# Routed experts behind linear attention: the first expert's first stage in seven products for two groups, and twelve sums on GpSimd

## The chip, the cores and the metric

One core of a Trainium2 chip runs the whole kernel. The time is device microseconds of one execution; the median of several runs is compared. The engines have their own instruction queues and work them off in order: TensorE (PE, matmuls), VectorE (DVE), ScalarE (ACT), GpSimd (POOL) and SyncE (SP, which only starts DMAs here). An instruction that waits for another engine holds everything behind it in its own queue.

## The reference

Eight heads of linear attention give x of 4608 rows and 512 columns. Routing turns x @ w_gate into a table P of 4608 x 8 by eight rounds of row and column scaling. Eight experts follow, and P weights their sum:

```python
logits = x @ w_gate
P = np.exp(logits - logits.max())
for _ in range(8):
    P /= P.sum(1, keepdims=True) + 1e-09
    P /= P.sum(0, keepdims=True) + 1e-09
    P *= N / E
for e in range(E):
    h = np.maximum(x @ w1[e], 0.0)
    out += P[:, e:e + 1] * (h @ w2[e])
```

N = 4608, D = 512, E = 8, F = 1024.

## The kernel before

x lies transposed in SBUF (`xT`, bf16) in nine groups of 512 rows; groups 0 to 7 form four pairs. The first stage of an expert is x @ w1 with relu (tile `hT`), the second is hT @ w2 (into `acc`, one f32 tile per group). The loop over experts is the last and longest part, some 775 of 1030 us.

Expert 0 works plainly: `up0` makes a quarter of a group's first stage (8 matmuls of 512 columns, 32 for the group), and `down0` one chunk of 128 rows of the second stage (8 matmuls of 512 columns, four chunks to a group). In the text a chunk is one such `down0`. Some of expert 0's work fills the attention stage; the rest runs behind it, in a list (`fill`) that alternates quarters and chunks. Beside it, on DVE and PE, runs the routing loop (`routing`).

Experts 1 to 7 use seven products instead of eight per group, each of a quarter of the operands (Winograd's scheme). That needs sums and differences made ahead: of w1 and w2 (`sums_w`, eight a expert, 128x1024 in bf16), and of x (`pair_sums_x` for a pair, `sums_x` for group 8), which are written to DRAM (`Xd`) and loaded again for each expert by `load_x`. `up7` is the first stage: products x1 to x4, y1, w1, w2 for each half `fp`; ACT keeps a partial result in SBUF (`keep`, tile `U`), DVE adds it to another and clips at zero (`add`), and one result goes through relu on ACT. For a single group a product is 4 matmuls of 256 columns and there are two halves, so 56 in all; for a pair it is 2 matmuls of 512 columns and four halves. `down7` is the second stage in seven products. `ORDER` interleaves the `up7` of one group with the `down7` of an earlier one. The second expert's first pair has no earlier one, so its products stand alone.

The routing loop has eight rounds, each a chain over two engines: DVE multiplies the table by `c_bc` (L952), sums its rows (L955), takes the reciprocal (L957), multiplies again (L958), sums columns into `cs` (L961); PE adds `cs` over the partitions (a matmul of 8 columns with `colw`, in the tile `early`); DVE takes the reciprocal into `c_bc` (L966). Both multiplications read two tensors in SBUF, of 288 f32 elements a partition. After the last round P is complete. P weights each expert's output, and the outputs of expert 0 are scaled by it on ACT at the start of `down7` of expert 1.

The order on each engine is not written by hand. Each operation is recorded with a duration that the author gave it, and a list scheduler (`Plan.schedule`) starts whatever can start earliest; the result is fixed at build time. An operation with `shared=True` doesn't overlap another such one in that plan: DVE's sums (`sub`) and the routing's multiplications have it, and everything on GpSimd.

GpSimd scales v in the attention stage, starts the loads of weights, and in the expert loop adds `V` to `acc` (L1317).

Of the kernel before, what the change touches and what calls it, by code (L numbers as in the profile page):

```python
# [228 lines left out]
def kernel(  # L229
# [11 lines left out]
    nc = tc.nc  # L241
# [93 lines left out]
    for x in range(2):  # L335
# [16 lines left out]
        late["s_p"].tile([128, 2, 512], BF16, name="X", tag=f"X_{i}"))  # L352
    ring("s_p", [128, NT], FP32, "rr", 1)
    ring("s_p", [128, E], FP32, "cs", 1)
    ring("s_p", [128, E], FP32, "c_bc", 1)
# [409 lines left out]
    def up(w1, g, hT, fcs, n, r=(), w=()):  # L765

        for f0 in fcs[::n]:
            ph = new(f"P{n}")
            ht = hT[f0 // 2]
            for i in range(n):  # L770
                for dc in range(NP):
                    pe(512, lambda f=f0 + i, i=i, dc=dc, ph=ph: mm(
                        ph()[:, 512 * i:512 * i + 512], w1()[:, dc, f * 128:(f + 1) * 128],
                        xT[:, dc, g * 512:(g + 1) * 512], dc == 0, dc == NP - 1),
                        xkeys(g, dc) + [(w1, (f0 + i) // 2), *r], [ph, *w], [ht])
            act(512 * n, lambda f0=f0, ph=ph, ht=ht: nc.scalar.activation(
                out=ht()[:, f0 % 2:f0 % 2 + n, :].rearrange("p a b -> p (a b)"),
                in_=ph()[:, 0:512 * n], func=ACT.Relu, bias=0.0, scale=1.0),
                [ph], [(ht, f0 + i) for i in range(n)])

    def down(w2, hT, tss, r=()):
        py = new(f"P{len(tss)}")
        for i, ts in enumerate(tss):
            for fc in range(8):
                pe(512, lambda i=i, ts=ts, fc=fc: mm(
                    py()[:, 512 * i:512 * i + 512],
                    hT[fc // 2]()[:, fc % 2, ts * 128:(ts + 1) * 128],
                    w2()[:, fc, :], fc == 0, fc == 7),
                    [(hT[f // 2], f) for f in (range(8) if fc == 0 else (fc,))]
                    + [(w2, f) for f in range(4)] + [*r], [(py, i)])  # L790
        return py
# [11 lines left out]
    def down0(g, part):  # L803
        tss = (part,)
        py = down(W[0][1], hts[g], tss, akey(g))

        def keys(ts):
            return [("acc", g, ts)] + [("acc", g, ts, j) for j in range(2) if g >= 9]
        for i, ts in enumerate(tss):
            if ts % 2:  # L810
                act(512, lambda i=i, ts=ts: nc.scalar.activation(
                    out=acc[g][:, ts, :], in_=py()[:, 512 * i:512 * i + 512], func=ACT.Copy,
                    bias=0.0, scale=P[:, 4 * g + ts, 0:1] if g >= 9 else 1.0),
                    [(py, i)] + akey(g), keys(ts))
# [87 lines left out]

    def expert0(i):
        if i < 4 * NG:
            up0(i // 4, i % 4)
        down0(i // 4 - 1, i % 4)

    fill = range(4 * NA + 4, 4 * NG + 4)

    def swap():  # L910
# [26 lines left out]
    def routing():  # L937
        c_bc = None
        for it in range(8):
            rr, wv, cs, pc = new("rr"), new("T"), new("cs"), new("P1")  # L940
            lk = [("L", g) for g in range(NG)]
            if c_bc is None:
                def u():
                    return L
                uk = lk
            else:
                ub = new("T")
                uk = [ub]

                def u(ub=ub):  # L950
                    return table(ub)
                dve(288, lambda u=u, c=c_bc: nc.vector.tensor_tensor(  # L952
                    out=u(), in0=L, in1=c()[:, None, :].to_broadcast([128, NT, E]),
                    op=ALU.mult), lk + [c_bc], uk, shared=True)
            dve(288, lambda u=u, rr=rr: nc.vector.tensor_reduce(  # L955
# [3 lines left out]
                out=table(wv), in0=L, in1=rr()[:, :, None].to_broadcast([128, NT, E]),  # L959
                op=ALU.mult), lk + [rr], [wv], shared=True)  # L960
            dve(480, lambda wv=wv, cs=cs: nc.vector.tensor_reduce(  # L961
# [7 lines left out]
            out=P, in0=table(wv), in1=c()[:, None, :].to_broadcast([128, NT, E]), op=ALU.mult),  # L969
            [c_bc, wv], ["P"], shared=True)  # L970

    routing()
    grant("X", 4, {id(d): d for key in [("L", g) for g in range(NG)] + ["colw"]
                   for d in plan.readers[key]}.values())
    for i in fill:
        expert0(i)


# [36 lines left out]
    def sums_w(e, w1, w2):  # L1015

        eng = pool if e == 0 else dve

# [14 lines left out]
        def t(n):  # L1033
# [32 lines left out]
        return A, Bq  # L1066

    def xq(g, i, j):

        return lambda: xT[:, 2 * i:2 * i + 2, 512 * g + 256 * j:512 * g + 256 * j + 256]  # L1070
# [7 lines left out]

    def pair_sums_x(p):

        X = [new("S") for _ in range(4)]

        def x(n):
# [3 lines left out]
        for n, y, z, r in ((0, b12, b11, ["sums of x"]), (1, b22, x(0), [X[0]]),  # L1087
                           (2, b22, b12, []), (3, b21, x(1), [X[1]])):
            sub(dve, 1024, x(n), y, z, ALU.subtract,
                xkeys(2 * p) + xkeys(2 * p + 1) + ["late"] + r,  # L1090
                [X[n]] + (["sums of x"] if n == 1 else []))
            dma("SP", 1 << 18, 250, lambda n=n: nc.sync.dma_start(out=Xd[p][n], in_=x(n)()),
                [X[n]], [("Xd", p, n)])

    def sums_x(g):

        X = [new("S") for _ in range(2)]

        def x(n):
            return lambda: X[n // 2]()[:, n % 2 * 2:n % 2 * 2 + 2]  # L1100

        b11, b12, b21, b22 = xq(g, 0, 1), xq(g, 0, 0), xq(g, 1, 1), xq(g, 1, 0)
        for n, y, z, r in ((0, b12, b11, []), (1, b22, x(0), [0]), (2, b22, b12, []),
                           (3, b21, x(1), [1])):
            sub(dve, 512, x(n), y, z, ALU.subtract,
                xkeys(g) + ["late", "sums of x"] + [(X[i // 2], i % 2) for i in r]
                + ([(X[1], "slot")] if n == 2 else []),
                [(X[n // 2], n % 2)] + ([(X[1], "slot")] if n == 0 else []))
        for i in range(2):
            dma("SP", 1 << 18, 250, lambda i=i: nc.sync.dma_start(  # L1110
                out=Xd[4][i], in_=X[i]().rearrange("p (k a) b -> p k (a b)", k=2)),
                [(X[i], n) for n in range(2)], [("Xd", 4, i)])

    def load_x(p):
# [19 lines left out]

    def up7(A, p, X, H, r0):

        pair = p < 4
        nf = 4 if pair else 2
        gs = (2 * p, 2 * p + 1) if pair else (8,)
        xk = [k for g in gs for k in xkeys(g)]  # L1140

        def b(n):
            i, j = {"11": (0, 1), "21": (1, 1), "22": (1, 0)}.get(n, (0, 0))
            if n[0] != "t":
                if pair:
                    return lambda k: xT[:, 2 * i + k, 1024 * p + 512 * j:][:, 0:512], []
                return lambda k: xT[:, 2 * i + k, 4096 + 256 * j:][:, 0:256], []
            t = int(n[1]) - 1
            if pair:
                return lambda k: X[t]()[:, k, :], [X[t]]  # L1150
            return lambda k: X[t // 2]()[:, t % 2, 256 * k:256 * k + 256], [X[t // 2]]

# [51 lines left out]
        more = [("banks", 0), ("banks", 1)]  # L1204
        more += [k for n in ("s2", "s3", "22") for k in A[n][1]] + X + list(r0)
        def x1(fp):
# [201 lines left out]
    ORDER = "X1 x10 w10 x11 X2 x20 y10 x21 Z1 y11 X3 w11 x30 x31 x40 x41 w20 Y1 w21 X4 Z2".split()  # L1408
    END = "aX1 aY1 b2 aX2 aZ1 b3 aX3 aX4 b0 aZ2 b1".split()
    queue = []  # L1410

    def pop():
        if not queue:
            return None
        e, g, H, B7, w2 = queue.pop(0)
        if (e, g) == (E - 1, 7):
            return down8(e, g, H, w2)
        return down7(e, g, H, B7)

    for e in range(1, E):  # L1420
# [63 lines left out]
```

## Time and profile before

| | us |
|---|---|
| runs | 1028.88, 1030.8, 1033.5 (median 1030.8) |
| the profiled execution | 1030.37 |
| its span, first to last instruction | 1028.6 |
| PE busy in it | 1006.3 |
| DVE, ACT, POOL busy | 866.7, 706.6, 465.1 |
| attention ends, routing starts | about 206 |
| P complete | 244.5 |
| first product of the second expert | 253.7 |

The profiled execution lies within the spread of the runs, 0.4 us under their median. Times in the trace are counted from the span's start. A row of the timeline has start, length, engine, line, operation, output <- inputs with shapes, a count, and in brackets the idle time before it and what ended it. A row of the grouped view has line, engine, operation, operands and count, then busy time and the mean in ns of one, then idle time before. Matmuls overlap their neighbours, so PE's pace is read from the distance of starts.

### The profile page before, as it was taken

To read this page: it belongs to the slowest core of one execution; us is meant where nothing else is said; L and a number is where in the kernel's file an instruction comes from. 1 tells how busy PE (TensorE), PEld (TensorE's weight loads), DVE (VectorE), ACT (ScalarE), POOL (GpSimd) and SP (SyncE) were. 2 spreads that over 40 slices of the span, in tenths; PEclk is the share of its full clock that TensorE was granted. 3 is DMA by queue.
4 is the path that set the end of the run, shared out by engine and by line. 5 is a ranking of instruction groups with operands and counts; after the bars stand their busy time and mean duration, and the time that the engine had idled before them with its cause. 6 is when DMAs were issued, how large, how long until landed. Compare 5 with 4: busy or idle time off the path is not lost.

```text
span 1028.6 us, 21737 instructions
## 1 busy us (share of the span) xinstructions
PE 1006.3 (98%) x7838; PEld 690.2 (67%) x7958; DVE 866.7 (84%) x1860; ACT 706.6 (69%) x1569; POOL 465.1 (45%) x534
## 2 busy tenths in 40 slices
PE   7899999999999999999999999999999999999998
PEld 5666666644566766676667766676667666776665
DVE  7999998987877888888878888888879888888776
ACT  7999999835688866656666566655666666665663
POOL 5877765400244353444434454435443544443443
PEclk9999999999999999999999999999999999999999
DMA  9998995095411243121611161106111341203333
GB/s 258 177 169 143 183 163 95 11 224 145 83 42 42 63 91 74 42 63 41 124 42 41 34 122 56 52 28 122 43 43 62 70 95 42 58 26 83 141 126 124
DMA packets 124316, 93.77 MB, mean 91 GB/s; under 512 B 47456, under 2 KB 115872, under 8 KB 124208
## 3 DMA queue, kind: packets, MB, share of 16 engines
q1 hardware_dynamic: 90448, 68.44, 24.5%
q0 software_dynamic: 33680, 23.90, 16.6%
q8 instruction: 62, 1.02, 0.4%
q14 instruction: 46, 0.38, 0.1%
q10 hardware_dynamic: 80, 0.03, 0.0%
HBM read 94.98 MB, written 14.16 MB: 106 GB/s over the span
## 4 chain that ended last, share of the span: by engine, by line
PE 91%; DVE 4%; DMA 1%; issue 1%; ACT 1%; SPq 0%; POOL 0%; DVEq 0%; ACTq 0%
PE P L1130 40%; PE P L1164 31%; PE P L484 18%; PE P L683 1%; DVE acc L1303 1%; DVE hT L1194 1%; DMA acc<-in_q_dram 1%; DVE w L1013 1%; PE P L722 1%; DMA acc<-in_k_dram 1%; DVE m L476 0%; SPq L406 0%; PE P L688 0%; DVE S L1013 0%; ACT k L480 0%
## 5 line engine op out<-in xcount | busy, mean ns | idle before, releaser
L1317 POOL TENSOR_TENSOR acc<-acc,V 128x512 f32<-128x512 f32 x244 | 313.9, 1298 | 433.4 <-ACT V L1313 430.0
L1190 ACT COPY U<-P 128x512 f32<-128x512 f32 x378 | 216.1, 588 | 133.4 <-PE P L1164 68.9
L1313 ACT ACTIVATE V<-P 128x256 f32<-128x256 f32 x488 | 212.7, 476 | 122.1 <-PE P L1130 118.6
L1194 DVE CUSTOM_DVE_ANT_0 hT<-P,U 128x512 bf16<-128x512 f32 x378 | 252.1, 686 | 36.7 <-ACT U L1190 21.0
L1130 PEld LDWEIGHTS <-S 128*128 128x128 bf16 x1984 | 194.1, 98 | 53.2
L1303 DVE SCALAR_TENSOR_TENSOR acc<-P,acc 128x256 f32<-128x256 f32 x372 | 159.6, 477 | 71.7 <-PE P L1130 69.2
L1164 PE MATMUL P<-xT,w 128*128 128x512 bf16 x682 | 193.3, 379 | 1.8 <-DVE acc L1303 0.6
L1130 PEld LDWEIGHTS <-hT 128*128 128x128 bf16 x1488 | 145.5, 98 | 55.8 <-DVE hT L1194 0.7
L1164 PE MATMUL P<-xT,T 128*128 128x512 bf16 x544 | 156.8, 379 | 1.6
L1130 PE MATMUL P<-w,hT 128*128 128x256 bf16 x992 | 143.7, 273 | 0.4 <-DVE hT L1194 0.3
L1130 PE MATMUL P<-T,S 128*128 128x256 bf16 x1056 | 137.0, 273 | 0.2
L1164 PEld LDWEIGHTS <-w 128*128 128x128 bf16 x896 | 87.6, 98 | 61.2 <-issue 0.7
L1130 PE MATMUL P<-w,S 128*128 128x256 bf16 x928 | 123.7, 273 | 1.1
L1013 DVE TENSOR_TENSOR S<-hT 128x512 bf16<-128x512 bf16 x248 | 104.7, 437 | 19.3 <-PE P L1130 18.3
L1164 PEld LDWEIGHTS <-T 128*128 128x128 bf16 x672 | 65.7, 98 | 58.0 <-issue 1.8
L609 POOL TENSOR_TENSOR v<-v_m,em 128x512 bf16<-128x512 f32 x64 | 67.0, 1046 | 42.7 <-ACT em L480 37.3
L476 DVE TENSOR_REDUCE m<-P 128x4 f32<-128x512 f32 x128 | 83.5, 677 | 3.1 <-PE P L484 1.6
L1199 ACT ACTIVATE hT<-P 128x512 bf16<-128x512 f32 x126 | 74.2, 598 | 11.7 <-PE P L1164 11.4
L484 PE MATMUL P<-w,hT 128*128 128x512 bf16 (+1 forms) x310 | 77.3, 373 | 0.9 <-DVE m L476 0.2
L484 PE MATMUL P<-xT,w 128*128 128x512 bf16 x271 | 71.7, 379 | 0.9 <-ACT q L480 0.3
L480 ACT ACTIVATE k<-P 128x512 bf16<-128x512 f32 x128 | 68.6, 628 | 2.3 <-PE P L484 1.4
L480 ACT ACTIVATE q<-P 128x512 bf16<-128x512 f32 x128 | 69.4, 639 | 0.4
(109 smaller groups left out, 1173.5 us busy)
## 6 DMA issues: line engine op xcount, KB each, us to landing
xT<-xd SPq DMA_DIRECT2D x168, 128.0 KB, 2.2
w<-in_moe_w_dram POOLq DMA_DIRECT2D x14, 1024.0 KB, 10.1
v_m<-in_v_dram SPq DMA_DIRECT2D x14, 512.0 KB, 4.8
out_dram<-acc SPq DMA_DIRECT2D x12, 512.0 KB, 3.1
X<-xd SPq DMA_DIRECT2D x42, 128.0 KB, 2.2
early<-xd SPq DMA_DIRECT2D x42, 128.0 KB, 2.2
xd<-S SPq DMA_DIRECT2D x18, 256.0 KB, 2.9
qk<-in_k_dram POOLq DMA_DIRECT2D x12, 256.0 KB, 5.2
```

The lines of the kernel that those rows point to most:

```text
L476: dve(el, lambda: nc.vector.tensor_reduce(out=dst(), in_=src(), axis=AX.X, op=ALU.max, apply_absolute_value=True), r, w)
L480: act(el, lambda: nc.scalar.activation(out=dst(), in_=src(), func=ACT.Exp, bias=0.0, scale=scale), r, w)
L484: nc.tensor.matmul(out_, lhsT=lhsT, rhs=rhs, start=start, stop=stop)
L1013: lambda: f.tensor_tensor(out=out_(), in0=x(), in1=y(), op=op), r, w, **kw)
L1130: pe(256, lambda i=i, k=k, z=z: nc.tensor.matmul(bank()[:, 256 * i:256 * i + 256], lhsT=lhs(k, i), rhs=rhs(k), start=first and z, stop=k = ...
L1164: pe(512, lambda k=k: nc.tensor.matmul(bank[fp](), lhsT=f()[:, k, 128 * fp:128 * fp + 128], rhs=rhs(k), start=first and k == 0, stop=k == ...
L1190: act(512, lambda: nc.scalar.copy(out=u[fp][n]().rearrange("p a b -> p (a b)"), in_=x[fp]()), [x[fp]], [u[fp][n]])
L1194: dve(500, lambda: nc.vector._custom_dve(ADD_SAT, out=out_(fp, i, j), in0=halves_(bank[fp]()), in1=flat(u[fp][n]()), s0=3.0e38, s1=0.0), [ ...
L1199: act(512, lambda: nc.scalar.activation(out=out_(fp, i, j), in_=halves_(x[fp]()), func=ACT.Relu, bias=0.0, scale=1.0), [x[fp]], [okey(fp, ...
L1303: dve(330, lambda n=n, ts=ts: nc.vector.scalar_tensor_tensor(out=acc[g][:, ts, 256 * j:256 * j + 256], in0=bank()[:, 256 * n:256 * n + 256 ...
L1313: act(390, lambda n=n: nc.scalar.activation(out=u()[:, n, :], in_=bank()[:, 256 * n:256 * n + 256], func=ACT.Copy, bias=0.0, scale=P[:, 4 ...
L1317: pool(670, lambda: nc.gpsimd.tensor_tensor(out=acc[g][:, 2 * i:2 * i + 2, 256 * j:256 * j + 256], in0=acc[g][:, 2 * i:2 * i + 2, 256 * j: ...
```

## The change

Expert 0's groups 7 and 8 go through `up7`: a new function `sums_w1_first` makes four sums of w1 on DVE, `sums_x` now also serves group 7 (in `T` buffers, kept in SBUF for this use, and only group 8's are written to DRAM). `FILL` puts group 6's quarters and two chunks ahead of it; `MIX` puts chunks of groups 5 and 6 between the products of groups 7 and 8; the chunks of groups 7 and 8 are queued like a `down7` and so stand between the first products of expert 1. Second-stage results of groups 5 to 8 all leave PSUM through ACT. Twelve sums move from DVE to GpSimd: those of x for pairs 2 and 3 (eight), and those of w2 for expert 1 (four). A one-column copy (`seen`) makes GpSimd start behind DVE's sums of pair 1. The routing's multiplications lose `shared=True` in the plan, and expert 1's sums no longer wait for P.

```diff
+    def hkeys(g, f):
+        return range(2) if g in (7, 8) else (f % 2,)
...
     def down0(g, part):
...
-            if ts % 2:
+            if ts % 2 or g > 4:
                 act(512, lambda i=i, ts=ts: nc.scalar.activation(
...
                 dve(288, lambda u=u, c=c_bc: nc.vector.tensor_tensor(
                     out=u(), in0=L, in1=c()[:, None, :].to_broadcast([128, NT, E]),
-                    op=ALU.mult), lk + [c_bc], uk, shared=True)
+                    op=ALU.mult), lk + [c_bc], uk)
...
     def sums_w(e, w1, w2):
-        eng = pool if e == 0 else dve
+        eng = dve
...
-        late = ["late"] + (["P"] if e == 1 else [])
+        late = ["late"]
...
         late = late + ["sums of w1"]
+        eng = pool if e == 1 else dve
...
+    def sums_w1_first():
+
+        w1 = W[0][0]
+        S = [new("T") for _ in range(4)]
+        wk = [(w1, n) for n in range(4)]
...
+        for n, y, z, op, r in ((0, q(0, 0), q(0, 1), ALU.add, []),
+                               (2, q(1, 0), q(0, 0), ALU.subtract, []),
+                               (1, s(0), q(1, 0), ALU.subtract, [S[0]]),
+                               (3, q(1, 1), s(1), ALU.subtract, [S[1]])):
+            sub(dve, 1024, s(n), y, z, op, wk + ["late"] + r, [S[n]])
...
-    def pair_sums_x(p):
+    def pair_sums_x(p, eng=dve):
         X = [new("S") for _ in range(4)]
+        if p == 2:
+            seen = new("seen")
+            pool(4, lambda: nc.gpsimd.tensor_copy(
+                out=seen()[:, 0:1], in_=pair_x[1][3]()[:, 3, 254:256].bitcast(FP32)),
+                [pair_x[1][3]], [seen, "sums of x"])
...
-            sub(dve, 1024, x(n), y, z, ALU.subtract,
+            sub(eng, 1024, x(n), y, z, ALU.subtract,
...
     def sums_x(g):
-        X = [new("S") for _ in range(2)]
+        X = [new("T") for _ in range(2)]
...
-    def up7(A, p, X, H, r0):
+    def up7(A, p, X, H, r0, g=8):
...
+    FILL = "u60 u61 u62 u63 d50 d51".split()
+    MIX = (("52", "53", "60"), ("61", "62", "63"))
...
+        if e == 0:
+            return lambda n: down0(g, CHUNK[n]) if n in CHUNK else None
...
+    CHUNK = {"X1": 0, "X2": 1, "Z1": 2, "Y1": 3}
+    routing()
...
+    A0 = sums_w1_first()
+    X0 = {7: sums_x(7), 8: sums_x(8)}
+    for p in range(4):
+        pair_sums_x(p, dve if p < 2 else pool)
+    for i in FILL:
+        (up0 if i[0] == "u" else down0)(int(i[1]), int(i[2]))
+    for g in (7, 8):
+        H = [[new("hT") for _ in range(2)] for _ in range(2)]
+        hts[g] = H[0] + H[1]
+        un = up7(A0, 5, X0[g], [H], ["late"], g)
...
+    queue += [(0, 7, None, None, None), (0, 8, None, None, None)]
...
-            for p in range(4):
-                pair_sums_x(p)
-            sums_x(8)
```

What the scheduler makes of it, on two engines. Line numbers in rows of the changed kernel are its own: L1003 is `sub` (L1013 before), L949 and L955 are the two multiplications of the routing (L952 and L958 before), L1221 is `add` (L1194 before).

GpSimd's queue in the kernel before, from the end of the attention stage to the first adds of the expert loop (`w_4274` and `w_4300` are w1 and w2 of expert 1, the next two those of expert 2):

```order
L641 COPY r<-r_r 128x2 x2
L378 DMA w_4274<-in_moe_w_dram 128x4x1024
L378 DMA w_4300<-in_moe_w_dram 128x8x512
L378 DMA w_4699<-in_moe_w_dram 128x4x1024
L378 DMA w_4767<-in_moe_w_dram 128x8x512
L1317 TENSOR_TENSOR acc_76<-acc_76,V 128x2x256 x4
```

The same place in the changed kernel, from the last two rows of the first six sums of x to the second load for expert 2 (`w_4706` and `w_4952` are w1 and w2 of expert 2):

```order
L1003 TENSOR_TENSOR S<-xT 128x1024
L1003 TENSOR_TENSOR S<-xT,S 128x1024
L379 DMA w_4706<-in_moe_w_dram 128x4x1024
L1003 TENSOR_TENSOR S<-xT 128x1024
L1003 TENSOR_TENSOR S<-xT,S 128x1024
L1003 TENSOR_TENSOR T<-w_4300 128x1024
L1003 TENSOR_TENSOR w_4300<-w_4300 128x4x256
L1003 TENSOR_TENSOR T<-w_4300 128x1024
L1003 TENSOR_TENSOR T<-w_4300,T 128x1024
L379 DMA w_4952<-in_moe_w_dram 128x8x512
```

Four more sums of x and the copy `seen` stand ahead of these; the load of expert 2's w1, which waits for the last product with expert 0's w1, now stands between the sixth and the seventh sum.

DVE's queue in the middle of the routing loop before, with sums of x between the steps of a round:

```order
L966 RECIPROCAL c_bc<-P 128x8
L1013 TENSOR_TENSOR S<-xT 128x1024
L952 TENSOR_TENSOR T<-early,c_bc 128x288
L818 COPY acc_4271<-P 128x512
L955 TENSOR_REDUCE rr<-T 128x36
L1013 TENSOR_TENSOR S<-xT,S 128x1024
L957 RECIPROCAL rr<-rr 128x36
```

And in the changed kernel, in rounds 5 to 7 of the loop (`w_4274` is w1 of expert 1):

```order
L955 TENSOR_TENSOR T<-early,rr 128x288
L1003 TENSOR_TENSOR T<-w_4274 128x1024
L958 TENSOR_REDUCE cs<-T 128x8
L963 RECIPROCAL c_bc<-P 128x8
L949 TENSOR_TENSOR T<-early,c_bc 128x288
L952 TENSOR_REDUCE rr<-T 128x36
L954 RECIPROCAL rr<-rr 128x36
L955 TENSOR_TENSOR T<-early,rr 128x288
L958 TENSOR_REDUCE cs<-T 128x8
L1003 TENSOR_TENSOR w_4274<-w_4274 128x2x512
L963 RECIPROCAL c_bc<-P 128x8
L1003 TENSOR_TENSOR T<-w_4274 128x1024
```

The sums of x have left these rounds, adds of the products of groups 7 and 8 (in other rounds) and expert 1's sums of w1 have come in; the loop itself ends later in the program, between the first products of expert 1. On PE the `cs` matmul of rounds 2 to 8 stands, counted in 512-column and 256-column matmuls behind the one before: 5 and 23 (to round 3's), 9 and 16 (4's), 18 and 16 (5's), 14 and 0 (6's), 26 and 0 (7's), 20 and 0 (8's).

More of the change, by code (lines that the diff above doesn't have):

```diff
@@ L778, in up, with down @@
                 in_=ph()[:, 0:512 * n], func=ACT.Relu, bias=0.0, scale=1.0),
-                [ph], [(ht, f0 + i) for i in range(n)])
-    def down(w2, hT, tss, r=()):
+                [ph], [(ht, (f0 + i) % 2) for i in range(n)])
+    def hkeys(g, f):
+        return range(2) if g in (7, 8) else (f % 2,)
+    def down(g, w2, hT, tss, r=()):
         py = new(f"P{len(tss)}")
@@ L969, in routing @@
             out=P, in0=table(wv), in1=c()[:, None, :].to_broadcast([128, NT, E]), op=ALU.mult),
[L970 to L976, printed above, removed]
+            [c_bc, wv], ["P"])
     def store(g, ts, js=(), nt=1):
@@ L1105, in sums_x, with view @@
             sub(dve, 512, x(n), y, z, ALU.subtract,
-                xkeys(g) + ["late", "sums of x"] + [(X[i // 2], i % 2) for i in r]
+                xkeys(g) + ["late"] + [(X[i // 2], i % 2) for i in r]
                 + ([(X[1], "slot")] if n == 2 else []),
                 [(X[n // 2], n % 2)] + ([(X[1], "slot")] if n == 0 else []))
-        for i in range(2):
+        def view(i):
+            return lambda: X[i]().rearrange("p (k a) -> p k a", k=2)
+        for i in range(2 if g == 8 else 0):
             dma("SP", 1 << 18, 250, lambda i=i: nc.sync.dma_start(
-                out=Xd[4][i], in_=X[i]().rearrange("p (k a) b -> p k (a b)", k=2)),
+                out=Xd[4][i], in_=view(i)()),
                 [(X[i], n) for n in range(2)], [("Xd", 4, i)])
+        return [(view(i), [(X[i], n) for n in range(2)]) for i in range(2)]
     def load_x(p):
@@ L1204, in up7 @@
         more = [("banks", 0), ("banks", 1)]
-        more += [k for n in ("s2", "s3", "22") for k in A[n][1]] + X + list(r0)
+        more += [k for n in ("s2", "s3", "22") for k in A[n][1]] + list(r0)
+        more += [k for _, key in X for k in key]
         def x1(fp):
@@ L1418, in pop @@
         return down7(e, g, H, B7)
+    CHUNK = {"X1": 0, "X2": 1, "Z1": 2, "Y1": 3}
+    routing()
+    grant("X", 4, {id(d): d for key in [("L", g) for g in range(NG)] + ["colw"]
+                   for d in plan.readers[key]}.values())
+    A0 = sums_w1_first()
[8 more added lines that the diff above has]
+        un = up7(A0, 5, X0[g], [H], ["late"], g)
+        mix = iter(MIX[g - 7])
+        for n in ORDER:
+            if len(n) == 3:
+                un[n[:2], int(n[2])]()
+            elif n in CHUNK:
+                i = next(mix, None)
+                if i:
+                    down0(int(i[0]), int(i[1]))
+    queue += [(0, 7, None, None, None), (0, 8, None, None, None)]
     for e in range(1, E):
```

37 lines of the change are left out of this document (23 added, 14 removed).

## The prediction

> **What bounds the kernel now.** I read the head of the page, then the stages, then who waits for whom.
>
> ```profile
> span 1028.6 us, 21737 instructions
> PE 1006.3 (98%) x7838; PEld 690.2 (67%) x7958; DVE 866.7 (84%) x1860; ACT 706.6 (69%) x1569; POOL 465.1 (45%) x534
> 200.00:250.00 50.00, 49.66 (x309) 24.96 (x312) 43.92 (x101) 23.94 (x44) 2.45 (x3) 1.00 0.68 174
> 250.00:300.00 50.00, 49.14 (x293) 28.80 (x296) 38.84 (x76) 35.12 (x70) 13.47 (x11) 1.00 0.37 80
> ```
>
> TensorE (PE) is busy 98% at full granted clock, so only matmul time and PE's waits count. The change lies between 206 and 270 us, in the last two rows (columns: length, then busy time and instructions of PE, PEld, DVE, ACT, POOL; clock; DMA). There PE idles 0.34 and 0.86 us: whoever speeds this stretch up can win little, whoever makes PE wait loses at once. GpSimd (POOL) is busy 2.45 us in the first 50: it rests while the routing loop runs.
>
> The loop is the second thing to see. One of its eight rounds on DVE, and the PE stretches beside it:
>
> ```profile
> 219.20 0.21 DVE L966 RECIPROCAL c_bc<-P 128x8 f32<-128x8 f32 x1 [0.55 <-PE P L484]
> 219.44 0.46 DVE L952 TENSOR_TENSOR T<-early,c_bc 128x288 f32<-128x288 f32 x1
> 219.94 0.45 DVE L955 TENSOR_REDUCE rr<-T 128x36 f32<-128x288 f32 x1
> 220.42 0.38 DVE L957 RECIPROCAL rr<-rr 128x36 f32<-128x36 f32 x1
> 220.84 0.46 DVE L958 TENSOR_TENSOR T<-early,rr 128x288 f32<-128x288 f32 x1
> 221.33 0.67 DVE L961 TENSOR_REDUCE cs<-T 128x8 f32<-128x288 f32 x1
> 221.92 0.68 DVE L1013 TENSOR_TENSOR S<-xT,S 128x1024 bf16<-128x1024 bf16 x1
> 222.54 0.21 DVE L966 RECIPROCAL c_bc<-P 128x8 f32<-128x8 f32 x1
> ...
> 206.03 0.94 PE L484 MATMUL P<-wgate,xT 128*128 128x8 bf16 x32
> 207.05 1.67 PE L484 MATMUL P<-w,hT 128*128 128x512 bf16 x7
> ...
> 240.12 0.28 PE L484 MATMUL P<-cs,early 128*128 128x8 f32 x2
> 240.25 1.89 PE L484 MATMUL P<-xT,w 128*128 128x512 bf16 x8
> 241.98 1.46 PE L484 MATMUL P<-w,hT 128*128 128x512 bf16 x6
> ```
>
> A round takes 222.54 - 219.20 = 3.34 us. Between `cs` and `c_bc` stands a small matmul (`cs,early`) in PE's own queue, and PE runs in order: where `cs` is late, all matmuls behind it wait. No PE wait for `cs` is reported now.
>
> **The change, part by part.**
>
> *Seven products.* Groups 7 and 8 lose 2 x 32 matmuls of 512 columns and get 2 x 56 of 256.
>
> ```profile
> 283.79 1.04 PE L1130 MATMUL P<-T,S 128*128 128x256 bf16 x8
> 284.66 0.59 PE L1164 MATMUL P<-early,T 128*128 128x512 bf16 x2
> ...
> 259.11 0.86 PE L1164 MATMUL P<-xT,w 128*128 128x512 bf16 x3 [0.24 <-ACT U L1190]
> 268.92 1.59 PE L1130 MATMUL P<-w,hT 128*128 128x256 bf16 x13 [0.31 <-DVE hT L1194]
> 253.74 0.38 PE L1164 MATMUL P<-xT,w 128*128 128x512 bf16 x1
> ```
>
> Eight of 512 columns take 241.98 - 240.25 = 1.73 us (0.216 each), eight of 256 take 0.87 (0.109). 64 x 0.216 = 13.84 leaves, 112 x 0.1087 = 12.18 comes: **-1.66 us**. The two waits of 0.24 and 0.31 stand where the second expert's first products run without filler; the moved output chunks fill them: **-0.5**, bounds 0 and -0.86.
>
> *DVE and ACT in bulk.* Rows for a sum, an add, an output copy on ACT and a load:
>
> ```profile
> 206.69 1.29 DVE L1013 TENSOR_TENSOR S<-xT 128x1024 bf16<-128x1024 bf16 x2 [0.40 <-DVE xT L725]
> 260.75 1.28 DVE L1194 CUSTOM_DVE_ANT_0 hT<-P,U 128x512 bf16<-128x512 f32 x2
> L811 ACT ACTIVATE acc<-P 128x512 f32<-128x512 f32 x8 | 4.8, 595 | 8.9 <-PE P L484 8.9
> xT<-xd SPq DMA_DIRECT2D x168, 128.0 KB, 2.2
> ```
>
> On DVE a sum of 1024, an add and a copy each cost about 0.6 us when they follow one another. It loses 8 copies, 8 pair sums and 4 sums of w2 and gets 12 adds, 4 sums of w1 and 4 of half size: about 1 us less. ACT takes the 8 copies, 8 x 0.6 = 4.8 us, and has 26 and 15 us free in the two stages. I cost both at nothing; what counts is order and waits.
>
> *Loads.* The two weight loads of expert 2 now stand behind sums on POOL's queue, some us later. PE wants them one expert later, (1028.6 - 253.7) / 7 = 111 us. On SP the third load of shifted x sits behind GpSimd's first sum, the fourth behind its fourth; that ends at 235.3 below, lands 2.2 us later and PE asks after 250. Covered by 12 us; a sum would have to take over 5 us to bare it.
>
> *Twelve sums on GpSimd.* No bf16 sum on GpSimd is in this trace. The nearest rows (x count, busy, mean ns):
>
> ```profile
> L1317 POOL TENSOR_TENSOR acc<-acc,V 128x512 f32<-128x512 f32 x244 | 313.9, 1298 | 433.4 <-ACT V L1313 430.0 <-DVE S L1013 1.1
> L609 POOL TENSOR_TENSOR v<-v_m,em 128x512 bf16<-128x512 f32 x64 | 67.0, 1046 | 42.7 <-ACT em L480 37.3 <-PE P L484 2.7 <-issue 1.5
> L542 POOL TENSOR_TENSOR vrd<-v_r,em_r 64x256 bf16<-64x256 f32 x32 | 19.5, 609 | 4.4 <-ACT em_r L480 2.8
> ```
>
> 256 more elements cost 1046 - 609 = 437 ns, 1.71 each with 0.17 us to start; the f32 add comes to 2.2 each. 1024 elements: 1.92 to 2.4 us. If bytes set the pace, a bf16 sum of 1024 costs what the f32 add of 512 does, 1.3; twice that add is 2.6. I take **2.1**, as these rows count elements, and keep 1.25 and 2.6 as ends. The Trainium skill's GPSIMD Engine Reference (Elementwise, side-by-side cycle accounting) counts 2.6 cycles an element for a two-input op at 1.2 GHz; by that estimate a sum takes 2.2 us and PE's waits below come to 12.1 instead of 10.9.
>
> Time on GpSimd is free. What it does to DVE isn't:
>
> ```profile
> 371.44 1.26 POOL L1317 TENSOR_TENSOR acc<-acc,V 128x512 f32<-128x512 f32 x1 [2.57 <-ACT V L1313]
> 371.60 1.38 DVE L1013 TENSOR_TENSOR S<-hT 128x512 bf16<-128x512 bf16 x1
> 395.75 2.67 POOL L1317 TENSOR_TENSOR acc<-acc,V 128x512 f32<-128x512 f32 x2 [2.58 <-ACT V L1313]
> 395.92 1.38 DVE L1013 TENSOR_TENSOR S<-S,hT 128x512 bf16<-128x512 bf16 x1
> 398.76 0.42 DVE L1013 TENSOR_TENSOR S<-hT,S 128x512 bf16<-128x512 bf16 x1
> ```
>
> A DVE sum of two SBUF tensors takes 0.42 us alone, but 1.38 when a GpSimd add began just before it: 371.60 + 1.38 = 372.98 is 0.28 behind that add's end (371.44 + 1.26). DVE is held for the whole of GpSimd's instruction, then gets one turn, also between two adds in a row (395.75).
>
> The loop's two multiplications (L952, L958) have two SBUF inputs too, and in the trace GpSimd rests beside them. Now it doesn't. The walk: PE has 45 matmuls of 512 behind 207.05 (9.7), then seven products (0.435 each) and two chunks (1.73) up to group 7's second add, 223.4. DVE's add, one multiplication and two sums with a reduction between end pair 1 at 226.2, and GpSimd starts at 226.6. From there a round's two multiplications each wait for the end of a sum. A sum and the turn behind it take 2.2 to 2.3 us:
>
> - Round 2: PE reaches its `cs` matmul at 229.4. The second multiplication comes at 227.1 and is held to 228.7; add and reduction follow, `cs` at 230.3. PE waits 0.9.
> - Round 3: PE's work to the next `cs` matmul is 23 matmuls of 256 and 5 of 512, 3.6 us. DVE: two adds, then both multiplications held (sums 3 and 4, to 233.1 and 235.3), `cs` after 6.0. Waits 2.4.
> - Round 4: 3.7 of work. Sums 5 and 6 (to 237.5, 239.7), an add, `cs` after 4.9. Waits 1.2.
> - Round 5: 5.6 of work. GpSimd stops for expert 2's load, which waits for group 8's last product; at 244.5 it goes on. Sum 7 holds the second multiplication, sum 8 the sum of w1 behind it: 8.7. Waits 3.1.
> - Round 6: 3.0 of work; sums 9 and 10; 4.5. Waits 1.5.
> - Round 7: 5.6 of work; sums 11 and 12 hold two sums of w1, the rest is free; 7.4. Waits 1.8.
> - Round 8: GpSimd is done, 4.3 against 4.3.
>
> Together **+10.9 us** (8.7 at 1.92 us a sum, 13.9 at 2.35, 16.9 at 2.6, 3.7 at 1.25). Later work moves as a block. Sum: -1.66 - 0.5 + 10.9 = +8.7 on the profiled execution's 1030.4, 1039.1; the median of the runs lies 0.4 above that execution: **1039.5**.
>
> **The rivals.**
>
> *Not slower: the multiplications aren't held.* Their kind is f32 with a broadcast input, the held rows are bf16; no row of this trace shows an f32 one beside GpSimd. Then only the four sums of w1 in rounds 5 to 7 are held, and by the same walk PE waits 0.95 us (1.25 a sum) to 4.4 (1.92), about 3 at 2.1: 1030.8 - 2.2 + 3 = 1031.6, and at most 1033. It decides at the input type. [...]
>
> *The sum costs 1.25 us.* For it: bf16 moves half the bytes. Against: L609 writes bf16 at the same pace per element. PE waits 3.7: 1032.3.
>
> *Nothing waits*, because the rounds find PE later than I think or DVE slips by: 1030.8 - 2.2 = 1028.6. Against it: the walk leaves no round but the last with room.
>
> *Worse:* sums at 2.6 us, or GpSimd taking two turns: 1045 and above.
>
> **How the numbers follow.** Forecast (1.9 to 2.4 us a sum, held: 1037.3 to 1042.5) 0.55; multiplications free 0.22; cheap sum 0.10; nothing waits 0.06; worse 0.07. The range, 1029 to 1044.5, has to take in the free multiplications, since without them over 2 in 10 would be left out. A measurement here tells about 0.5%, 5.2 us, from no change. Faster needs under 1025.6, which no term gives: 0.02. Slower (over 1036): forecast and worse, less a little: 0.60. Same: 0.38.
>
> **What would show it.** Seven products: PE's busy time down by some 1.7 us. Sums: POOL rows of 128x1024 at about 2.1 us from 226 on. Holding: `T<-early` rows of 1 to 2.5 us instead of 0.46, and PE waits for DVE `cs` of 1 to 3 us, six of them. I am wrong if those rows stay at 0.46, if GpSimd starts after the loop, or if PE waits elsewhere (for `U`, for X loads).

## The result, and the profile after

| | before | after |
|---|---|---|
| median of 6 runs each, us | 1030.24 | 1041.51 |
| lowest to highest, us | 1028.88 to 1033.5 | 1041.19 to 1042.25 |
| profiled execution, us | 1030.37 | 1041.46 |
| its span, us | 1028.6 | 1039.7 |

The ratio is 1.0107, with an interval of 1.0092 to 1.0122: the changed kernel is about 1% slower. All of it is lost between 206 and 280 us; from there on DVE's rows lie 11.1 us later than before, to the end. The head of the page after, then the two stages as before (length, busy time and instructions of PE, PEld, DVE, ACT, POOL; clock; DMA):

```profile
span 1039.7 us, 21990 instructions
...
PEclk9999999998999999999999999999999999999999
```

```profile
200.00:250.00 50.00, 44.94 (x335) 27.21 (x331) 42.77 (x79) 21.90 (x41) 21.42 (x13) 0.97 0.66 164
250.00:300.00 50.00, 44.89 (x254) 25.49 (x255) 42.97 (x77) 31.36 (x62) 16.36 (x12) 0.93 0.34 74
```

PE idles 5.06 and 5.11 us where it idled 0.34 and 0.86, and the granted clock, 1.00 before, is 0.97 and 0.93. There are two losses, waits and clock. PE's timeline of the changed kernel shows both (start, length, engine, line, operation, operands, count, in brackets the idle time before):

```profile
229.49 0.60 PE L1154 MATMUL P<-xT,T 128*128 128x256 bf16 x4 [0.64 <-DVE hT L1221]
...
236.37 0.36 PE L485 MATMUL P<-cs,early 128*128 128x8 f32 x2 [2.30 <-DVE cs L958]
236.58 2.30 PE L485 MATMUL P<-w,hT 128*128 128x512 bf16 x6
238.67 1.06 PE L1154 MATMUL P<-xT,w 128*128 128x256 bf16 x4
239.53 1.93 PE L1154 MATMUL P<-T 128*128 128x256 bf16 x12
241.29 0.81 PE L485 MATMUL P<-w,hT 128*128 128x512 bf16 x3
...
254.30 0.56 PE L485 MATMUL P<-cs,early 128*128 128x8 f32 x2 [6.43 <-DVE cs L958]
254.72 4.55 PE L485 MATMUL P<-w,hT 128*128 128x512 bf16 x14
259.11 0.28 PE L485 MATMUL P<-cs,early 128*128 128x8 f32 x2
...
268.56 0.38 PE L1191 MATMUL P<-xT,T 128*128 128x512 bf16 x1 [0.81 <-DVE hT L1221]
```

The waits are 0.64 + 2.30 + 6.43 + 0.81 = 10.2 us. Behind the two long ones the matmuls run slower. Fourteen of 512 columns take 259.11 - 254.72 = 4.39 us instead of 14 x 0.216 = 3.02; six of 512 and sixteen of 256 take 241.29 - 236.58 = 4.71 instead of 1.30 + 1.74 = 3.04. Together that is 3.0 us. The seven products and the two filled waits were put at -2.2: 10.2 + 3.0 - 2.2 = 11.0, against 11.1 in the spans.

Why `cs` is late stands in DVE's rows (the multiplications are L949 and L955 now):

```profile
226.94 1.90 DVE L955 TENSOR_TENSOR T<-early,rr 128x288 f32<-128x288 f32 x1
...
229.36 0.66 DVE L958 TENSOR_REDUCE cs<-T 128x8 f32<-128x288 f32 x1
...
231.37 1.85 DVE L949 TENSOR_TENSOR T<-early,c_bc 128x288 f32<-128x288 f32 x1
...
234.15 1.36 DVE L955 TENSOR_TENSOR T<-early,rr 128x288 f32<-128x288 f32 x1
235.55 0.67 DVE L958 TENSOR_REDUCE cs<-T 128x8 f32<-128x288 f32 x1
...
240.63 0.66 DVE L958 TENSOR_REDUCE cs<-T 128x8 f32<-128x288 f32 x1
...
242.96 0.45 DVE L949 TENSOR_TENSOR T<-early,c_bc 128x288 f32<-128x288 f32 x1
...
245.24 5.81 DVE L955 TENSOR_TENSOR T<-early,rr 128x288 f32<-128x288 f32 x1
250.98 2.60 DVE L1003 TENSOR_TENSOR T<-w 128x1024 bf16<-128x1024 bf16 x1
```

and beside them in GpSimd's:

```profile
226.40 2.12 POOL L1003 TENSOR_TENSOR S<-xT 128x1024 bf16<-128x1024 bf16 x1
228.60 2.23 POOL L1003 TENSOR_TENSOR S<-xT,S 128x1024 bf16<-128x1024 bf16 x1
230.78 2.12 POOL L1003 TENSOR_TENSOR S<-xT 128x1024 bf16<-128x1024 bf16 x1
232.86 2.33 POOL L1003 TENSOR_TENSOR S<-xT,S 128x1024 bf16<-128x1024 bf16 x1
...
243.63 0.80 POOL L379 DMA_DIRECT2D w<-in_moe_w_dram  x1 [3.85 <-PE P L1154]
244.45 2.14 POOL L1003 TENSOR_TENSOR S<-xT 128x1024 bf16<-128x1024 bf16 x1
246.54 2.12 POOL L1003 TENSOR_TENSOR S<-xT,S 128x1024 bf16<-128x1024 bf16 x1
248.62 2.11 POOL L1003 TENSOR_TENSOR T<-w 128x1024 bf16<-128x1024 bf16 x1
250.81 2.22 POOL L1003 TENSOR_TENSOR w<-w 128x1024 bf16<-128x1024 bf16 x1
```

The multiplication of 226.94 ends at 228.84, 0.3 us after GpSimd's sum of 226.40 has ended: it was held. At 242.96 GpSimd rests, and the loop's other multiplication takes 0.45. The one of 245.24 is the new thing. It should have got in at 246.6, behind the sum of 244.45. It missed that end and the next, and ended at 251.05, behind the third: 5.81 us for 0.45 of work. PE waited 6.43 us for the `cs` that follows it. The sum of w1 behind it was then held for one sum more (2.60).

### The profile page after: what moved, and what is told of

It reads as the page before. It is cut to its first block, busy times and chain, and to the rows that moved or that the text cites. A ratio compares the mean times of both kernels' runs of the same rounds, so it can differ in the third digit from the quotient of the medians.

```text
span 1039.7 us, 21990 instructions
## 1 busy us (share of the span) xinstructions
PE 1013.6 (97%) x8006; PEld 695.5 (67%) x8006; DVE 879.2 (85%) x1860; ACT 709.4 (68%) x1577; POOL 491.9 (47%) x547
## 4 chain that ended last, share of the span: by engine, by line
PE 90%; DVE 7%; ACT 2%; issue 1%; DMA 0%; POOL 0%; DVEq 0%; ACTq 0%; POOLq 0%
PE P L1154 40%; PE P L1191 31%; PE P L485 16%; PE P L684 1%; DVE hT L1221 1%; DVE T L955 1%; ACT k L481 1%; DVE acc L1331 1%; DVE m L477 1%; DVE w L1003 1%; ACT q L481 1%; PE P L723 1%; DVE T L949 0%; DMA wphi_f<-in_w_phi_dram 0%; PE P L689 0%
## 5 line engine op out<-in xcount | busy, mean ns | idle before, releaser
L1217 ACT COPY U<-P 128x512 f32<-128x512 f32 x390 | 222.8, 587 | 139.4 <-PE P L1191 106.4
L1221 DVE CUSTOM_DVE_ANT_0 hT<-P,U 128x512 bf16<-128x512 f32 x390 | 260.3, 687 | 41.8 <-ACT U L1217 19.4
L1191 PE MATMUL P<-xT,w 128*128 128x512 bf16 x728 | 201.0, 379 | 0.6 <-DVE acc L1331 0.6
L1191 PE MATMUL P<-xT,T 128*128 128x512 bf16 x560 | 160.9, 379 | 0.8 <-DVE hT L1221 0.8
L1003 DVE TENSOR_TENSOR S<-hT 128x512 bf16<-128x512 bf16 x248 | 104.9, 439 | 19.3 <-PE P L1154 18.3
L1226 ACT ACTIVATE hT<-P 128x512 bf16<-128x512 f32 x130 | 76.7, 598 | 13.8 <-PE P L1191 12.4
L485 PE MATMUL P<-w,hT 128*128 128x512 bf16 (+1 forms) x328 | 83.7, 382 | 0.2 <-DVE m L477 0.2
L1154 PE MATMUL P<-T,hT 128*128 128x256 bf16 x496 | 66.4, 273 | 0.0
```

What stands on the lines that cost most here:

```text
L485: nc.tensor.matmul(out_, lhsT=lhsT, rhs=rhs, start=start, stop=stop)
L1003: lambda: f.tensor_tensor(out=out_(), in0=x(), in1=y(), op=op), r, w, **kw)
L1154: pe(256, lambda i=i, k=k, z=z: nc.tensor.matmul(bank()[:, 256 * i:256 * i + 256], lhsT=lhs(k, i), rhs=rhs(k), start=first and z, stop=k = ...
L1191: pe(512, lambda k=k: nc.tensor.matmul(bank[fp](), lhsT=f()[:, k, 128 * fp:128 * fp + 128], rhs=rhs(k), start=first and k == 0, stop=k == ...
L1217: act(512, lambda: nc.scalar.copy(out=u[fp][n]().rearrange("p a b -> p (a b)"), in_=x[fp]()), [x[fp]], [u[fp][n]])
L1221: dve(500, lambda: nc.vector._custom_dve(ADD_SAT, out=out_(fp, i, j), in0=halves_(bank[fp]()), in1=flat(u[fp][n]()), s0=3.0e38, s1=0.0), [ ...
```

## The experiments

Each time below is the median, and each ratio is to the kernel before on the same chip (1030.5 to 1030.7 us). Line numbers differ a little from kernel to kernel.

**The multiplications lose their second SBUF input.** The routing's small tables `rr` and `c_bc` go to a bank of PSUM; the orders of PE and GpSimd stay as in the changed kernel.

```diff
-            rr, wv, cs, pc = new("rr"), new("T"), new("cs"), new("P1")
+            wv, cs = new("T"), new("cs")
...
-                dve(288, lambda u=u, c=c_bc: nc.vector.tensor_tensor(
-                    out=u(), in0=L, in1=c()[:, None, :].to_broadcast([128, NT, E]),
+                dve(288, lambda u=u: nc.vector.tensor_tensor(
+                    out=u(), in0=L, in1=cc()[:, None, :].to_broadcast([128, NT, E]),
                     op=ALU.mult), lk + [c_bc], uk)
```

Here `cc` is a slice of the tile `pc`, which lies in PSUM.

> The routing's small tables (row sums and c_bc) lie in PSUM instead of SBUF; the order on PE and GpSimd is that of the changed kernel, to the row. Theory (a DVE op with two SBUF inputs is held by GpSimd's sums): the 15 multiplications fall back to about 0.46 us each, also the one of 5.81; only the four sums of w1 can still be held; PE's waits for cs shrink from 8.7 to 0 to 3 us, and the time to 1030 to 1033. Rival (the rounds are late for another reason, as their place in DVE's queue or f32 operands as such): multiplications of 1 to 6 us remain and the time stays at 1040 to 1042.

1034.75 us, ratio 1.0038 (1.0023 to 1.0053). The groups of multiplications (count, busy time, mean ns of one), first in the changed kernel, then with the tables in PSUM:

```profile
L955 DVE TENSOR_TENSOR T<-early,rr 128x288 f32<-128x288 f32 x8 | 12.2, 1528 | 0.1
L949 DVE TENSOR_TENSOR T<-early,c_bc 128x288 f32<-128x288 f32 x7 | 6.1, 872 | 0.1
```

```profile
L963 DVE TENSOR_TENSOR T<-early,P 128x288 f32<-128x288 f32 x8 | 3.6, 445 | 0.1
L957 DVE TENSOR_TENSOR T<-early,P 128x288 f32<-128x288 f32 x7 | 3.1, 449 | 0.1
```

The same multiplications with one input in PSUM are no longer held, and about 7 of the 11 us come back. The cause of these holds is the second SBUF input. The time is still 1.8 us above the theory's range. What is left hangs on one row of DVE and the wait that it makes on PE:

```profile
240.38 6.23 DVE L1011 TENSOR_TENSOR T<-w 128x1024 bf16<-128x1024 bf16 x1
```

```profile
247.25 0.60 PE L485 MATMUL P<-cs,early 128*128 128x8 f32 x2 [4.67 <-DVE cs L966]
```

A sum of w1, still with two SBUF inputs, now stands where a multiplication stood, and is held for 6.23 us through three sums.

**No sums on GpSimd.** All twelve are on DVE again; w2's stand behind P, as before the change.

```diff
-        late = late + ["sums of w1"]
-        eng = pool if e == 1 else dve
+        late = late + ["sums of w1"] + (["P"] if e == 1 else [])
...
-        pair_sums_x(p, dve if p < 2 else pool)
+        pair_sums_x(p)
```

> All twelve sums are back on DVE (expert 1's sums of w2 behind P again), everything else is as in the changed kernel. Theory (GpSimd's sums cost the time, the seven products and the moved chunks gain 1.66 to 2.5): 1028 to 1030, no multiplication over 0.5 us, no PE wait for cs over 0.5. Rival (the routing loop's later end, or the new products' order, costs too): 1033 or more, with PE waits that are not behind GpSimd.

1035.51 us, ratio 1.0043 (1.0028 to 1.0057). Nothing is held, and still it is slower than before, as the rival had it. PE's only wait there, and DVE's queue ahead of the add that it waits for:

```profile
234.27 1.01 PE L1153 MATMUL P<-xT,T 128*128 128x256 bf16 x4 [3.99 <-DVE hT L1220]
```

```profile
227.84 0.68 DVE L1003 TENSOR_TENSOR S<-xT 128x1024 bf16<-128x1024 bf16 x1
...
233.54 0.68 DVE L1220 CUSTOM_DVE_ANT_0 hT<-P,U 128x512 bf16<-128x512 f32 x1
```

Six sums of x stand between 227.84 and the add of group 7 at 233.54, and PE waits 3.99 us for that add, with half the clock behind it. So the adds that the seven products bring and the sums of x don't fit on DVE in this order. Taking the sums away from DVE has its use; what hurts is what GpSimd does to DVE.

**A pause behind each sum, with a new order.** A copy of one column on GpSimd reads each sum's result, so that the next sum can't be ready while one runs. Here the copies are operations of the plan, and the order changed with them.

```diff
+            pool(4, lambda: nc.gpsimd.tensor_copy(out=turn()[:, 0:1], in_=last()),
+                 [w[0]], [turn, "turn of sums"])
```

> Behind each of the twelve sums GpSimd copies one column of its result (0.2 us), so that the next sum can't be queued up before the last one is complete. Theory (DVE lost its turn three times in a row, 5.81 us, because the next sum was waiting already and depended on nothing): no multiplication over 2.4 us, PE waits for cs in every round but none over 3.5 us, 1036 to 1040. Rival (who gets the turn is not a matter of the next sum's readiness): a multiplication of 4 us or more remains, 1041 to 1044 with the copies' time.

1041.87 us, ratio 1.0101 (1.0086 to 1.0116). The longest hold of a multiplication is 2.28 us, so none loses its turn. But PE waits in more rounds, 2.60, 3.37, 1.44 and 1.20 us for `cs` and 2.0 in three other places, 10.6 in all. The order had moved too, so this run couldn't say what the lost turns alone are worth. (In the changed kernel the instruction of 5.81 us lost two turns in a row, not three as the expectation has it.)

**The plan knows of the shared inputs again.** `shared=True` is back on the routing's multiplications, and the scheduler keeps them clear of GpSimd's sums in its own reckoning.

```diff
-                    op=ALU.mult), lk + [c_bc], uk)
+                    op=ALU.mult), lk + [c_bc], uk, shared=True)
```

> The plan again counts the routing's multiplications as excluding GpSimd's sums (shared=True on all three); nothing else is changed, the scheduler makes another order from it. If the cost came from a plan that didn't know of the holding, 1029 to 1033. If the holding comes whatever the plan counts, as nothing makes GpSimd wait for a multiplication on the chip, several multiplications of 1 to 2.3 us remain: 1035 to 1042.

1047.15 us, ratio 1.0157 (1.0142 to 1.0172), the slowest of all and 5 us above the higher of the two ranges. DVE's timeline has a hold of the same size as before:

```profile
242.15 5.80 DVE L949 TENSOR_TENSOR T<-early,c_bc 128x288 f32<-128x288 f32 x1
```

PE waits 5.76 and 3.58 us for `cs`. An order planned without overlap has the overlap on the chip all the same, since the engines don't keep to the plan's times.

**The pause alone.** The copy is now issued in the same planned operation as the sum, so that the order on every engine is that of the changed kernel.

```diff
+        def fn():
+            f.tensor_tensor(out=out_(), in0=x(), in1=y(), op=op)
+            if eng is pool:
+                t = out_()
+                nc.gpsimd.tensor_copy(out=turn[0]()[:, 0:1], in_=t[
+                    :, t.shape[1] - 1, t.shape[2] - 2:t.shape[2]].bitcast(FP32))
```

> The changed kernel with the order of every engine kept, and one short copy on GpSimd behind each of the twelve sums that reads that sum's result, so that the next sum cannot be started while the one before is still running. Theory (DVE's held instruction loses its turn only when GpSimd's next sum is already waiting behind the running one): no multiplication of the routing loop is held for more than one sum (at most 2.4 us; 5.81 in the changed kernel), PE's wait of 6.43 us falls to 1 to 3 us, the half clock behind it is gone or shorter; time 1034 to 1038. Rival (the loss is the sum of single holds and only lies elsewhere): PE's waits add up to 10 us again, time 1040 to 1043.

1039.53 us, ratio 1.0086 (1.0071 to 1.0101). No multiplication is held for more than 2.23 us. In the round that had 5.81 the multiplication again comes 0.8 us into a sum (at 247.69, the sum began at 246.91); it gets in behind that sum, after 1.68 us, and PE waits 0.39 there instead of 6.43. The longest of PE's remaining waits for `cs` and for an add:

```profile
237.46 0.57 PE L485 MATMUL P<-cs,early 128*128 128x8 f32 x2 [2.81 <-DVE cs L958]
262.39 0.59 PE L1200 MATMUL P<-xT,w 128*128 128x512 bf16 x2 [1.68 <-DVE hT L1230]
```

With 0.39 and 1.36 for `cs` and 0.63 and 0.97 for two other adds that is 7.8 us, and from 236.8 to 243.7 the clock is halved. So both theories were half right: the lost turns go, as the first said, and single holds cost PE most of the time anyway, as the second said. The time lies between their figures, 2 us below the changed kernel, with intervals that still overlap.

**Both together.** Tables in PSUM, and the pause.

> The kernel with the routing's small tables in PSUM, with the same short copies on GpSimd behind each sum and the same order on every engine. Theory: the sum of w1 (T<-w) that was held 6.23 us is held at most 2.4, PE's wait of 4.67 us for cs falls to 1 or less, no half clock; time 1028.5 to 1031, so about 4 to 6 us less than without the copies. Rival (that sum is held by something other than lost turns, for instance by GpSimd's reads of w): it stays at 5 us or more and the time at 1034 to 1036.

1031.56 us, ratio 1.0009 (0.9999 to 1.0019), against 1.0038 without the pause: 3 us, with intervals apart; it is 0.6 us above the range expected. The sum of w1 held 6.23 takes 0.69, and PE waits for no `cs`. That isn't a turn kept, though, as the row and GpSimd's seventh sum show:

```profile
239.54 0.69 DVE L1014 TENSOR_TENSOR T<-w 128x1024 bf16<-128x1024 bf16 x1
```

```profile
240.30 2.14 POOL L1014 TENSOR_TENSOR S<-xT 128x1024 bf16<-128x1024 bf16 x1
```

Without the pause DVE's sum came 0.59 us behind the start of the seventh sum (240.38 and 239.79). With it, six copies stand ahead of the seventh sum, and DVE's comes 0.76 ahead of it and is through. So the copies bring 3 us with the order unchanged, but in this place by moving the meeting. What kept turns alone bring is shown only by the run with the pause alone, with 2 us and intervals that overlap. Two other sums of w1 now meet the sums of w2 on GpSimd. Each gets in behind one sum, and PE waits for an add behind them; DVE first, then PE:

```profile
245.37 2.64 DVE L1014 TENSOR_TENSOR T<-w 128x1024 bf16<-128x1024 bf16 x1
...
248.29 2.38 DVE L1014 TENSOR_TENSOR T<-w,T 128x1024 bf16<-128x1024 bf16 x1
```

```profile
252.10 0.59 PE L1208 MATMUL P<-xT,w 128*128 128x512 bf16 x2 [2.38 <-DVE hT L1238]
```

The profiled execution (1028.97 us) was the fastest of ten; the trace shows what is left at its mildest.

**One part alone.** The kernel before, with only the eight sums of x for pairs 2 and 3 on GpSimd, and no seven products.

```diff
-                pair_sums_x(p)
+                pair_sums_x(p, dve if p < 2 else pool)
```

> The kernel before, with one part of the change alone: the eight sums of x for pairs 2 and 3 on GpSimd; plain first stage, its old order, w2's sums on DVE. Theory (the move to GpSimd costs by itself, wherever the products stand): GpSimd's sums lie beside rounds 5 to 8 of the loop, multiplications there are held 1 to 6 us, PE waits for cs 3 to 8 us in all; time 1033 to 1039. Rival (the move costs only together with the seven products, because they leave PE less work between two cs matmuls): PE waits under 1 us, time 1029 to 1032.

1037.75 us, ratio 1.0067 (1.0051 to 1.0083). One of DVE's multiplications and the longest of PE's waits:

```profile
225.25 2.36 DVE L958 TENSOR_TENSOR T<-early,rr 128x288 f32<-128x288 f32 x1
```

```profile
228.46 0.36 PE L484 MATMUL P<-cs,early 128*128 128x8 f32 x2 [1.84 <-DVE cs L961]
```

Four waits for `cs` add up to 5.1 us, and the clock falls once. The move to GpSimd costs by itself, without the seven products. One thing came out otherwise than expected: GpSimd, which has no copy here that starts it behind DVE's sums, began at 208, and the waits are in rounds 1 to 4 instead of 5 to 8. Of the 8.7 us in the span some 1 us isn't traced.

**Fewer sums on GpSimd.** Tables in PSUM, no pause, and only the eight sums of x moved; w2's stay on DVE behind P.

> The changed kernel with the routing's small tables in PSUM and only the eight sums of x on GpSimd; w2's four sums for the second expert stand on DVE again, behind P. Theory: the multiplications are free (0.45 us), a sum of w1 is held for one to three sums of x, PE waits for cs 0 to 3 us; time 1029 to 1032. Rival (DVE is the bound of this stretch once it has the w2 sums again): PE waits for adds on DVE 2 to 4 us, time 1033 to 1036.

1033.22 us, ratio 1.0026 (1.0017 to 1.0035). One sum of w1 is held 4.19 us, through two sums, and PE waits 2.62 for `cs`. PE's other waits for DVE are 0.46 (an add) and 0.53 (`acc`), not 2 to 4: DVE isn't the bound with w2's sums. The time came out 1.2 us above the theory's range, in the rival's, but without the waits that the rival named. With the pause added to this kernel:

> The kernel with the routing's small tables in PSUM and only the eight sums of x on GpSimd, with the short copy behind each of those sums; the order of every engine is that of the run without the copies. Theory: the 4.19 us for which a sum of w1 was held falls to 2.4 or less, PE's wait of 2.62 us for cs goes; 1.0 to 1.5 us of waits for adds on DVE stay; time 1029 to 1031.5. Rival (the copies only move the wait): PE waits 2 us or more in another round, time 1032 to 1034.

1030.42 us, ratio 0.9997 (0.9989 to 1.0006): the hold goes, PE waits 0.41 + 0.46 + 0.18 us, and the pause is worth some 3 us again (1.0026 to 0.9997). Here too the meeting has moved: the sum of w1 that came 0.57 us behind the start of GpSimd's seventh sum (240.60 and 240.03) comes 0.77 ahead of it (240.85 and 241.62).

**The last meeting taken away.** All twelve sums on GpSimd, tables in PSUM, the pause, and one more copy that makes GpSimd's sums of w2 start behind DVE's last sum of w1.

```diff
+            if first:
+                t = first()
+                nc.gpsimd.tensor_copy(out=turn[0]()[:, 0:1], in_=t[:, 1022:1024].bitcast(FP32))
...
+        if e == 1:
+            gate_w.append(S[3])
```

> The kernel with the routing's small tables in PSUM and a short copy behind each of the twelve sums, with one more copy that makes GpSimd's w2 sums start behind DVE's last sum of w1 (in the run without it they met: two sums of w1 were held 2.64 and 2.38 us, and PE waited 2.38 us for an add behind them). Theory: those two are back at 0.7 us, PE's wait of 2.38 goes, no PE wait over 0.5 us from 200 to 262; the w2 sums now lie beside the next expert's sums on DVE, which are held 1 to 2.4 us, off PE's path; time 1027.5 to 1030.5. Rival (the holds then hit sums that PE needs, S<-hT): PE waits 1 to 3 us between 255 and 275, time 1030.5 to 1033.

1027.20 us (1026.55 to 1027.8), ratio 0.9963 (0.9949 to 0.9977). This is faster than both kernels, and 0.3 us below the range expected. Its span is 1026.0 us. Its two stages:

```profile
200.00:250.00 50.00, 49.66 (x378) 30.55 (x381) 41.19 (x96) 24.80 (x46) 22.56 (x22) 1.00 0.72 176
250.00:300.00 50.00, 49.63 (x306) 30.47 (x312) 43.05 (x87) 40.17 (x80) 21.92 (x19) 1.00 0.32 78
```

PE idles 0.34 and 0.37 us, no wait of PE is reported, no multiplication or sum of w1 is held, and the clock is full. The span is 2.6 us under that of the kernel before. That is the change as it was meant: what the seven products and the fillers bring once GpSimd's sums hold nothing that PE waits for.

## Why the prediction was right, and where it was not

The predicted 1039.5 lies 2.0 us under the measured 1041.5, which is inside the likeliest case (1037.3 to 1042.5). Its steps:

- **Seven products and filled waits, -2.2 us.** The kernel without these meetings is 2.6 us under the kernel before in the span and 3.4 by the medians, so the sign holds and the size is somewhat more. That kernel has the tables in PSUM as well; the products alone were not measured. The sign named for it, PE's busy time down by 1.7, can't be read: the busy time rose from 1006.3 to 1013.6, with the halved clock in it, and the trace of before has 120 matmul records fewer than weight loads.
- **A sum on GpSimd takes 2.1 us.** Measured 2.11 to 2.43, from 226.40 on (predicted 226.6). The rivals of 1.25 and 2.6 fall.
- **Multiplications are held.** Shown by the run with the tables in PSUM. The rival that f32 multiplications go free, at 22%, falls. The Trainium skill, SBUF — State Buffer (Who interferes with whom), says that a VectorE instruction with two SBUF inputs contends with a GpSimd instruction that reads SBUF; these rows agree (1528 and 872 ns with both inputs in SBUF, 445 and 449 with one in PSUM).
- **The step that failed: DVE "then gets one turn, also between two adds in a row".** Up to round 4 the walk is right: it has `cs` at 230.3, 236.3 and 241.2 (round 2, then 6.0 and 4.9 later), and DVE's rows of `cs` end at 230.0, 236.2 and 241.3. Its waits there, 0.9 + 2.4 + 1.2 = 4.5, came as 0.64 for an add, 2.30 for `cs` and 1.7 more for matmuls at half the clock, behind which the wait of round 4 disappears: 4.6. In round 5 the walk let one sum hold the multiplication and one the sum of w1. DVE lost two turns, four sums held the two, and PE waited 6.43 instead of 3.1.
- **What made up for it.** The waits of 1.5 and 1.8 in rounds 6 and 7 did not come: the ninth and tenth sum had run in round 5, and the eleventh held nothing that PE waited for. The twelfth held a multiplication of round 8 for 1.64 us (at 265.42), where the walk had GpSimd done, and PE waited 0.81 for the add behind it. Two waits for `cs` came where six were named. From round 5 on PE lost 6.43, 1.4 at half the clock and these 0.81, 8.6 in all, where the walk had 6.4. That these are so near each other is luck, for the walk has the rounds wrong here.
- **The term that is missing: the clock.** 3.0 us of PE at half rate stood in no part of the sum; 1.2 of them lie where the walk had the wait of round 4. With them PE lost 13.2 us, against the 10.9 of the walk. These 2.3 us are the miss: the profiled execution was put at 1039.1 and took 1041.46.
- **Loads, bulk of DVE and ACT, at nothing.** No PE wait for a load or for `acc` is reported in this stretch. The run without sums on GpSimd qualifies the costing of DVE: with the twelve back on DVE, PE waits 3.99 us for an add. The text said that order and waits count there, and gave them no price.

## What to carry to other kernels

Work that moves from VectorE to GpSimd still costs VectorE, wherever both read SBUF and VectorE's operation has two SBUF inputs: look for a short instruction of that kind on the path that another engine waits for, before asking how much time the move frees. Three repairs helped here and added up: one of the two inputs in PSUM (about 7 us), a short copy behind each of GpSimd's long operations (2 to 3 us, in part because it moved a meeting), and a real dependency that keeps the two engines' meetings off the path (some 5 us). Knowing of the conflict in the plan did not help.

## What the runs showed of the hardware

**A lost turn.** A held DVE instruction does not always get in when GpSimd's instruction ends. Where GpSimd's next sum depends on the one just running, or a copy stands between them, the held one got in each time: in the changed kernel behind the sums of 226.40, 235.16 and 248.62 (the sum of 250.81 overwrites what the one before it reads), and in the three runs with the pause in which anything was held. Where the next sum depended on nothing recent, it got in four times (in the changed kernel behind the sums of 230.78 and 232.86, twice in the run with `shared=True`) and missed seven ends: two each in the changed kernel, with `shared=True` and with the tables in PSUM, one with fewer sums. All seven are ends of the first or second sum behind a weight load that GpSimd had started, as at 243.63; the four are not. What decides between these isn't settled.

**Half the clock after a short wait.** The changes of granted clock in the trace stand on a grid of 3.413 us. Three pairs or triples of such windows (columns as above): of the changed kernel, the one in which the 2.30 us wait lies and the one behind it; of the kernel before with one part of the change, around its wait of 1.84 us; and of the run with fewer sums and no pause, around its wait of 2.62 us:

```profile
233.64:237.05 3.41, 1.11 (x7) 0.48 (x6) 3.27 (x7) 0.62 (x2) 3.41 (x2) 1.00 0.47 167
237.05:240.47 3.42, 3.42 (x14) 1.77 (x13) 3.32 (x5) 0.60 (x1) 2.66 (x2) 0.50 0.41 142
```

```profile
226.59:230.00 3.41, 1.56 (x10) 0.85 (x10) 2.81 (x5) 0.04 (x1) 0.71 (x1) 1.00 0.00 0
230.00:233.42 3.42, 3.42 (x10) 1.22 (x9) 3.39 (x8) 1.15 (x2) 0.00 (x0) 0.50 0.50 165
```

```profile
240.77:244.19 3.42, 2.04 (x10) 0.72 (x8) 3.42 (x1) 0.60 (x1) 3.42 (x2) 1.00 0.97 129
244.19:247.60 3.41, 2.18 (x11) 1.12 (x12) 2.79 (x7) 0.60 (x1) 0.04 (x1) 1.00 1.01 181
247.60:251.01 3.41, 3.41 (x18) 1.61 (x17) 3.38 (x8) 1.19 (x2) 0.00 (x0) 1.00 0.77 239
```

The two shorter waits leave PE busy for 33% and 46% of one window, and the next one runs at half the clock. The longest falls across two windows, which are busy for 60 and 64%, and the clock stays. I worked this share out for every window of the twelve profiled executions from 30 us on, from the matmul rows. At full clock, nine windows have PE busy for 0 to 46%; behind each of them the clock is halved. Behind none with 49% or more it is. So the length of a wait doesn't decide alone; how much of one window it takes does. This is read from traces, not tried by an experiment of its own. The Trainium skill, TensorE: Matmul & The Clock Gate (Part 1: The HAM clock gate), gives half the rate after at least one idle window of about 3.4 us; the window's length agrees, but here a window that was busy for 46% was idle enough, and a wait of 1.84 us did it.
